# Copying y of the first two units on ScalarE alone, and putting back products that only the next half needs

## The chip, the cores and the metric

The kernel runs on one core of a Trainium2 chip. A core has TensorE (PE, matrix products, with its weight loads listed as PEld), VectorE (DVE), ScalarE (ACT), GpSimd (POOL) and SyncE (SP, which here only issues DMAs). Each works through its own queue in order; semaphores tie the queues together. The metric is the device time in microseconds (us), the median of the runs.

## The reference

A gated linear attention, and behind it a bilinear feed-forward layer. The attention has batch 4, 8 heads, 768 tokens and head size 48:

```python
f = 1.0 / (1.0 + np.exp(-f_logit))
for t in range(S):
    state = f[:, :, t, :, None] * state + np.einsum('bhd,bhe->bhde', k[:, :, t], v[:, :, t])
    y[:, :, t] = np.einsum('bhd,bhde->bhe', q[:, :, t], state)
x = y.transpose(0, 2, 1, 3).reshape(B * S, H * D)
out = ((x @ w_a) * (x @ w_b)) @ w_out
```

x has 3072 rows of 384 channels, and w_a, w_b are 384 x 1536, w_out 1536 x 384. The weights come in as doubles and are turned into 32-bit floats on the chip.

## The kernel before

**Units.** The attention is cut into 16 units: 4 batches, 2 halves of 384 tokens each, 2 groups of 4 heads. Units 0 and 1 (FIRST) are the two head groups of the first half of batch 0; unit 2 and 3 are the same heads in the second half. A unit is cut into chunks of 128 tokens (c from 0 to 2, for n of 2 pairs of heads), and each chunk into two pieces of 64 (p is 0 or 1). Step j = 2c + p goes from 0 to 5.

**Stages of a unit.** The front (front_parts, L313) has four parts: two sigmoids on ScalarE and an affine step on GpSimd; running products of f by a scan on VectorE (L333, one per n) with a small comparison; running sums of the inverse by six scans (L346); and k and q multiplied by them (L350). Then on TensorE: scores (L396), turn (L421, a transpose of k, copied by ScalarE in turned), gains (L445, what each piece adds to the state, one PSUM bank for each p), within (L504, y from the same piece) and across (L530, y from the state before the piece). VectorE masks the scores (L409) and adds up states from the gains (carry, L472 and L474). out_of_bank (L553) copies y out of PSUM, and stores_of (L575) sends it by DMA into xT, the transposed input of the feed-forward part. For unit 0 these stores alternate between SP's and POOL's queues, for unit 1 (u == NQ - 1) they go round ACT, SP and POOL.

Step j = 5 of carry makes the state behind the last piece. Only the next half of the same heads reads it, by way of hand_on, which comes after up(0, 1) in program order.

**The feed-forward part.** up(blk, ft) is 6 calls, 12 matmul records, of x with 128 columns of w_b and w_a (L619). Each call of a 32-bit matmul shows as two records with two weight loads. product copies one factor on ScalarE (L640) and multiplies on VectorE (L645). up(0, 0, True) goes by tiles of xT: the first needs unit 0 alone, the second both units, the third unit 1.

**Weights.** Pieces of the weights are loaded by SP (load_weights, L269) and converted by from_double: begin puts two passes on ScalarE (L71, L72), one on GpSimd (L73), and then a third on ScalarE (L75); end puts the last on VectorE (L78, and L83 three times for w_a and w_b). up(0, 0) needs pieces 0 and 1, up(0, 1) and up(0, 2) pieces 2 and 3, up(0, 3) and up(0, 4) pieces 4 and 5.

**The order.** The head of the kernel, up to the end of unit 3, is written out by hand (L1030 to L1148): every call puts its instructions on the queues in program order. The rest is placed by a planner that works from fixed costs and doesn't see the head. PSUM is ps_x, ps_y (two banks each, one tile for both) and four single banks ps_f, given out by the list idle. turn of a FIRST unit takes two of them, carried gives them back after its last step, and up takes two. keep_up issues products with no use, to a bank that is free.

In the head before, unit 1's within takes two ps_f banks, y of unit 1 is copied in four parts that alternate between ScalarE and VectorE (line 552), and the first scan of unit 2 stands ahead of y of unit 1, the second behind it (L1075 to L1081).

Of the kernel before, what the change touches and what calls it, by code (L numbers as in the profile page):

```python
# [22 lines left out]
BLK = 384  # L23
# [6 lines left out]
R = 64  # L30
SUB = 64
# [78 lines left out]
def kernel(  # L110
# [29 lines left out]
    with ExitStack() as pools:  # L140
        again, ending = by_quotients(pools, tc, q, k, f_logit, v, moe_w_a, moe_w_b, moe_w_out, out, ident, weights, bad, banks)
# [12 lines left out]
def by_quotients(ctx, tc, q, k, f_logit, v, moe_w_a, moe_w_b, moe_w_out, out, ident, weights, bad, ps_f):  # L154
    nc = tc.nc
    B, H, D, S = q.shape
# [4 lines left out]
    NQ = H // 4  # L161
    NC = BLK // C
    NJ = BLK // SUB
# [5 lines left out]
    FIRST = range(NQ)  # L169
# [42 lines left out]
    def unit(u):  # L212
        b, r = divmod(u, NH * NQ)
        return (b, *divmod(r, NQ))
# [57 lines left out]
    def begin(n):  # L272

        while 2 * n > begun[0] < 2 * len(todo):
            i, second = divmod(begun[0], 2)
            dst, src, shape = todo[i]
            if not second:
                going.append(
                    from_double(
                        nc, dst, raws[i], shape[0], next(blocks), bits[i % len(bits)], some, whole, shape[0] == NKT  # L280
                    )
                    if src.dtype != FP32 else iter(())
                )
            next(going[i], None)
            begun[0] += 1
# [19 lines left out]
    live = {}  # L305
    firsts = groups[:, len(EARLY)].rearrange("p (u n s) -> p u n s", u=NQ, n=2)
    products_of_f = {u: firsts[:, u] if u in FIRST else sets[u % NSET]["f"] for u in range(NU)}
# [52 lines left out]
    ps_x, ps_y = (ps_a.tile([128, 2, 512], FP32, tag=n, name=n) for n in ("ps_x", "ps_y"))  # L360
    idle = list(range(4))
# [5 lines left out]
    def each():  # L367
        for n in range(2):
            for c in range(NC):
                yield n, c, (n * NC + c) * SUB  # L370

    def give_back(ps):
        idle.extend(i for x in ps for i, bank in enumerate(ps_f) if bank is x)


    def home(u):

        return ps_y if u in (1, 3) else ps_x
# [5 lines left out]
    def pair_of(x):  # L384

        return [x[:, i] for i in range(2)]
# [17 lines left out]
    def mask(u):  # L404

        at = sb1.tile([128, 2, BLK], FP32, tag="at", name="at")
        to, x = (y.rearrange("s h (o t) -> s h o t", t=SUB) for y in (at, home(u)[:, :, 0:BLK]))
        tri = causal.unsqueeze(1).unsqueeze(1)
        nc.vector.tensor_tensor(to, x, tri.broadcast_to((128, 2, 2 * NC, SUB)), ALU.mult)  # L409
        live[u]["at"] = at  # L410
# [18 lines left out]
        else:  # L429
            nc.scalar.copy(kT.rearrange("s n c x -> s n (c x)"), away(u)[:, :, 0:NC * (R + D)])  # L430

    def gains(u, chunks=range(NC)):

        _, half, _ = unit(u)
        t, kT = sets[u % NSET], live[u]["kT"]
        last = half == NH - 1
        ps = live[u]["turned"]
        for n in range(2):
            for c in chunks:
                for p in range(2):  # L440
                    if last and c == NC - 1 and p == 1:
                        continue
                    for h in range(2):
                        r = slice(SUB * p, SUB * p + SUB)
                        nc.tensor.matmul(  # L445
                            ps[p][R * h:R * h + D, (n * NC + c) * D:(n * NC + c) * D + D],
                            lhsT=kT[r, n, c, R * h:R * h + D],
                            rhs=t["v"][r, n, c, h * D:h * D + D],
                            start=True,
                            stop=True,  # L450
                        )
        if chunks[0]:
            return
        st = sb3.tile([128, NJ, 2, D], FP32, tag="st", name="st")
        before = live[u - NQ]["st"][NJ] if half else None
        live[u]["st"] = [before] + [st[:, j] for j in range(NJ - 1 if last else NJ)]

    def carried(u, js=range(NJ)):

        for j in js:  # L460
            if j + 1 < len(live[u]["st"]):
                carry(u, j)
        if js[-1] == NJ - 1:
            give_back(live[u]["turned"])

    def carry(u, j):

        before, st = live[u]["st"][j:j + 2]
        c, p = divmod(j, 2)
        new = live[u]["turned"][p][:, 0:2 * NC * D].rearrange("r (n c d) -> r n c d", n=2, c=NC)[:, :, c]  # L470
        if before is None:
            nc.vector.tensor_copy(st, new)  # L472
        else:
            nc.vector.tensor_tensor(st, before, new, ALU.add)  # L474
# [16 lines left out]
    def within(u):  # L491

        t, at = sets[u % NSET], live[u]["at"]
        if u == NQ - 1:

            ps = live[u]["y"] = [ps_f[idle.pop(0)] for _ in range(2)]
        else:
            ps = live[u]["y"] = pair_of(home(u) if u < 2 * NQ else ps_y)
        for n, c, o in each():
            for p in range(2):  # L500
                for h in range(2):
                    r = slice(SUB * p, SUB * p + SUB)
                    e = R * (p ^ h)
                    nc.tensor.matmul(  # L504
                        ps[p][e:e + D, o:o + SUB],
                        lhsT=t["v"][r, n, c, h * D:h * D + D],
                        rhs=at[r, h, o:o + SUB],
                        start=o == 0,
                        stop=True,
                        skip_group_check=True,  # L510
                    )

    def across(u):

        b, half, qd = unit(u)
        qf, st, ps = halves(sets[u % NSET]["q"]), live[u]["st"], live[u]["y"]

        order = [(n, c, o, p) for n, c, o in each() for p in range(2)]
        if u in FIRST:

            order = sorted(order[::-1], key=lambda x: -x[3])
        elif half:
            order = [(n, c, o, p) for n, c, o in reversed(list(each())) for p in range(2)]
        for n, c, o, p in order:
            j = 2 * c + p
            if j == half == 0:
                continue
            for h in range(2):
                r, e = slice(R * h, R * h + D), R * (p ^ h)
                nc.tensor.matmul(  # L530
                    ps[p][e:e + D, o:o + SUB],
                    lhsT=st[j][r, n],
                    rhs=qf[r, tokens(n, c, p)],
                    start=False,
                    stop=True,
                    skip_group_check=True,
                )

    def out_of_bank(u, part):

        if "y_sb" not in live[u]:
            if u == NQ - 1:

                live[u]["y_sb"] = groups[:, 2 * NTG - 1, PIECE:].rearrange("r (o p m) -> r o p m", p=2, m=SUB)
            else:
                live[u]["y_sb"] = sb1.tile([128, 2 * NC, 2, SUB], FP32, tag="y", name="y")
        if u == NQ - 1:

            p, e, r, rows = ((1, R, 0, D), (0, 0, 0, D), (1, 0, R, D), (0, R, R, D))[part]
        else:  # L550
            p, e, r, rows = ((1, R, 0, D), (1, 0, R, D), (0, 0, 0, 128))[part if u in FIRST else part - 1]
        copy = nc.vector.tensor_copy if u == NQ - 1 and part % 2 else nc.scalar.copy
        copy(live[u]["y_sb"][r:r + rows, :, p], live[u]["y"][p][e:e + rows, 0:BLK].rearrange("r (o m) -> r o m", m=SUB))  # L553

    def stored(u):

        for do in stores_of(u):
            do()
# [440 lines left out]
    with tc.manual_schedule():  # L999
# [9 lines left out]
        parts = {u: front_parts(u) for u in range(2 * NQ)}  # L1009

        def emit_all(steps):
            for _, _, do, *args in steps:
                do(*args)

        def keep_up(n, to, width=BLK):


            x = products_of_f[0][:, 0, 0:width]
            for _ in range(n):
                nc.tensor.matmul(to[:, 0:width], lhsT=ident, rhs=x, start=True, stop=True)  # L1020

        def y_of(u):
            for part in range(4 if u == NQ - 1 else 3):
                out_of_bank(u, part)
            stored(u)
            if u == NQ - 1:
                give_back(live[u]["y"])


        for u in FIRST:  # L1030
# [30 lines left out]
        emit_all(parts[2][0])  # L1061
        begin(2.5)
        gains(1, range(NC - 1))
        carried(0)
        mask(1)
        carried(1, range(1))

        within(1)
        gains(1, range(NC - 1, NC))
        across(0)  # L1070
        keep_up(1, ps_y[:, 0], SUB)
        y_of(0)
        end(1)
        carried(1, range(1, NJ - 1))
        first_scan, *scans = parts[2][1]  # L1075
        emit_all([first_scan])
        across(1)
        keep_up(2, ps_y[:, 0])
        y_of(1)
        carried(1, range(NJ - 1, NJ))  # L1080
        emit_all(scans)  # L1081
        begin(3)
        end(2)
        emit_all(parts[2][2])


        load_unit(3, "f")
# [600 lines left out]
```

## Time and profile before

| | |
|---|---|
| runs | 589.22, 589.61, 590.11 us; median 589.61 |
| profiled execution | 590.78 us, its span 588.9 us |
| PE busy | 568.4 us, 97% of the span |
| PEld busy | 510.7 us, 87% |
| DVE busy | 412.0 us, 70% |
| ACT busy | 257.5 us, 44% |
| POOL busy | 90.4 us, 15% |
| head, 20.00 to 40.34 us | PE busy 14.97 us, DVE 16.12, ACT 13.87 of 20.34 |
| 40.34 us to the end | PE busy 544.27 of 548.56 us |

The span runs from the first to the last instruction of one profiled execution. In a line of a timeline the first number is the start in us from the span's start, the second the duration, then engine, source line, operation, what is written and read, and how many records are merged. In brackets stands the idle time of the engine ahead of it, and what ended it; "issue" means that the profile shows nothing that the engine waited for. A q behind an engine's name is its sequencer, which issues DMAs.

### The profile page before, as it was taken

What the parts mean: (1) busy time and instruction counts of PE and PEld (TensorE: products, weight loads), DVE (VectorE), ACT (ScalarE), POOL (GpSimd) and SP (SyncE); (2) the same over time, 40 slices, a digit from 0 to 9 for tenths busy, and PEclk for the clock granted to TensorE, in tenths of its full rate; (3) what the DMA queues carried; (4) which work ended last, traced back from release to release, by engine and by line L of the source; (5) the groups of instructions that cost most, each with busy time, mean ns of one, the idle gap of its engine ahead of it and who ended that gap; (6) DMA issues with size and microseconds to landing.
All of it is one profiled execution on the core that took longest, in us unless ns stands there. A gap on an engine that the chain in (4) does not pass through costs nothing.

```text
span 588.9 us, 13930 instructions
## 1 busy us (share of the span) xinstructions
PE 568.4 (97%) x5796; PEld 510.7 (87%) x5796; DVE 412.0 (70%) x782; ACT 257.5 (44%) x494; POOL 90.4 (15%) x73
## 2 busy tenths in 40 slices
PE   2789999999999999999999999999999999999997
PEld 1546655558999999999999999999999999999997
DVE  6799644599878869876997777837785165836651
ACT  5587668652122554246520444326431345235400
POOL 7365456454000000000000000000000000000000
PEclk9999999999999999999999999999999999999999
DMA  8789489089444123034105400041001100000001
GB/s 198 200 237 303 133 241 297 20 151 186 102 133 107 52 53 102 1 90 100 43 2 129 119 11 2 2 113 36 3 1 48 48 2 0 2 28 0 1 29 32
DMA packets 33576, 49.42 MB, mean 84 GB/s; under 512 B 3984, under 2 KB 25280, under 8 KB 33504
## 3 DMA queue, kind: packets, MB, share of 16 engines
q1 hardware_dynamic: 30000, 42.19, 26.2%
q0 software_dynamic: 3088, 5.92, 5.9%
q8 instruction: 47, 0.77, 0.6%
q10 hardware_dynamic: 416, 0.34, 0.2%
q14 instruction: 25, 0.20, 0.1%
HBM read 33.23 MB, written 4.72 MB: 64 GB/s over the span
## 4 chain that ended last, share of the span: by engine, by line
PE 91%; DVE 5%; issue 2%; ACT 1%; DMA 1%; SPq 0%; DVEq 0%; ACTq 0%
PE ps_f L745 39%; PE ps_f L847 28%; PE ps_f L619 15%; PE ps_y L504 2%; PE ps_y L530 2%; PE ps_x L445 1%; PE ps_x L396 1%; PE ps_x L421 1%; DVE inv L346 1%; DVE q_in L350 1%; DVE groups L333 1%; DMA f_in<-in_f_logit_dram 1%; DVE at L409 0%; DVE groups L737 0%; DVE spare L346 0%
## 5 line engine op out<-in xcount | busy, mean ns | idle before, releaser
L619 PE MATMUL ps_f<-xT,w_ba 128*128 128x384 f32 x288 | 95.8, 490 | 0.7 <-DVE w_ba L83 0.6
L1335 ACT COPY sums<-ps_f 128x384 f32<-128x384 f32 x120 | 57.6, 480 | 76.2 <-PE ps_f L745 68.5
L619 PEld LDWEIGHTS ps_f<-xT,w_ba 128*128 128x128 f32 x288 | 53.7, 190 | 37.8 <-ACT spare L75 1.2
L1335 ACT COPY groups<-ps_f 128x384 f32<-128x384 f32 x120 | 57.6, 481 | 61.3 <-PE ps_f L745 40.7
L745 PE MATMUL ps_f<-xT,w_ba 128*128 128x192 f32 x384 | 78.5, 327 | 0.0
L745 PEld LDWEIGHTS ps_f<-xT,w_ba 128*128 128x128 f32 x384 | 64.7, 190 | 0.3
L73 POOL TENSOR_SCALAR sums<-sums 128x768 f32<-128x768 f32 (+1 forms) x20 | 52.6, 2629 | 34.5 <-ACT sums L71 34.4
L745 PE MATMUL ps_f<-groups,w_ba 128*128 128x192 f32 x288 | 54.9, 326 | 0.0
L745 PE MATMUL ps_f<-x_sums,raw 128*128 128x192 f32 x288 | 53.7, 330 | 0.5 <-DVE groups L737 0.5
L329 POOL TENSOR_SCALAR inv<-inv 128x768 f32<-128x768 f32 x14 | 13.6, 972 | 261.2 <-ACT inv L326 217.0
L847 PE MATMUL ps_f<-w_out,sums 128*128 128x192 f32 x288 | 51.9, 327 | 0.0
L847 PE MATMUL ps_f<-w_out,groups 128*128 128x192 f32 x288 | 51.8, 329 | 0.0
L847 PE MATMUL ps_f<-spare,sums 128*128 128x192 f32 x288 | 49.5, 327 | 0.0
L745 PEld LDWEIGHTS ps_f<-x_sums,raw 128*128 128x128 f32 x288 | 47.0, 190 | 2.6 <-ACT sums L1335 1.0
L745 PEld LDWEIGHTS ps_f<-groups,w_ba 128*128 128x128 f32 x288 | 48.0, 190 | 0.1
L847 PEld LDWEIGHTS ps_f<-w_out,groups 128*128 128x128 f32 x288 | 47.2, 190 | 0.7
L847 PEld LDWEIGHTS ps_f<-w_out,sums 128*128 128x128 f32 x288 | 47.3, 190 | 0.2
L847 PEld LDWEIGHTS ps_f<-spare,sums 128*128 128x128 f32 x288 | 47.0, 190 | 0.1
L737 DVE TENSOR_TENSOR sums<-ps_f,sums 128x384 f32<-128x384 f32 x60 | 32.7, 553 | 16.9 <-PE ps_f L745 12.9
L737 DVE TENSOR_TENSOR sums<-sums,groups 128x768 f32<-128x768 f32 x36 | 34.3, 953 | 11.8 <-ACT groups L1335 11.2
L745 PE MATMUL ps_f<-xT,raw 128*128 128x192 f32 x192 | 39.4, 328 | 0.2 <-ACT groups L1335 0.2
L745 PE MATMUL ps_f<-x_sums,w_ba 128*128 128x192 f32 x192 | 39.3, 327 | 0.0
(150 smaller groups left out, 850.7 us busy)
## 6 DMA issues: line engine op xcount, KB each, us to landing
raw<-w_ba POOLq DMA_DIRECT2D x11, 512.0 KB, 8.3
k_in<-in_k_dram SPq DMA_DIRECT2D x32, 144.0 KB, 4.4
q_in<-in_q_dram SPq DMA_DIRECT2D x32, 144.0 KB, 4.5
v_in<-in_v_dram SPq DMA_DIRECT2D x16, 288.0 KB, 5.1
raw<-in_moe_w_out_dram SPq DMA_DIRECT2D x6, 768.0 KB, 4.8
out_dram<-o SPq DMA_DIRECT2D x22, 192.0 KB, 1.9
f_in<-in_f_logit_dram SPq DMA_DIRECT2D x28, 144.0 KB, 3.0
xT<-y SPq DMA_DIRECT2D x44, 72.0 KB, 2.1
```

The source lines that it names most:

```text
L73: nc.gpsimd.tensor_scalar(h, h, HI_MIN, HI_MAX, ALU.max, ALU.min)
L329: nc.gpsimd.tensor_scalar(inv, inv, EXP_K, 1.0, ALU.mult, ALU.add)
L333: nc.vector.tensor_tensor_scan(F[:, c], F[:, c], none, math.exp(MIDDLE), ALU.mult, ALU.add)
L346: nc.vector.tensor_tensor_scan(inv[:, w], inv[:, w], none[:, 0:C], first, ALU.mult, ALU.add)
L350: nc.vector.tensor_tensor(halves(t[nm]), halves(t[nm]), by, ALU.mult)
L504: nc.tensor.matmul(ps[p][e:e + D, o:o + SUB], lhsT=t["v"][r, n, c, h * D:h * D + D], rhs=at[r, h, o:o + SUB], start=o == 0, stop=True, ski ...
L530: nc.tensor.matmul(ps[p][e:e + D, o:o + SUB], lhsT=st[j][r, n], rhs=qf[r, tokens(n, c, p)], start=False, stop=True, skip_group_check=True,)
L619: nc.tensor.matmul(ps[nm][:, 0:BLK], lhsT=w[:, kt, ft * 128:ft * 128 + 128], rhs=xT[blk][:, kt], start=kt == 0, stop=kt == NKT - 1,)
L737: nc.vector.tensor_tensor(to, x, y, op)
L745: nc.tensor.matmul(ps[:, g], lhsT=sums_of_w[name][:, g, 128 * j:128 * j + 128], rhs=sums_of_x[blk][name], start=start and g == 0, stop=Tru ...
L847: nc.tensor.matmul(to, lhsT=x[:, i // 2, i % 2], rhs=w[:, NI * (i % 2) + i // 2], start=start and i == 0, stop=i == HFT - 1, skip_group_ch ...
L1335: do(*args)
```

## The change

Four edits, all in the head:

- Unit 1's within writes ps_y instead of two ps_f banks. Its y is copied in three parts, all on ScalarE, as unit 0's is: first the two parts with 48 rows of bank p = 1, then the 128 rows of bank p = 0.
- The gains of unit 1's last chunk are split by p. Those of p = 0 stay; those of p = 1, which feed step j = 5 alone, go behind across(1). gains gets an argument for it.
- The last carry of unit 0 goes behind the scans of unit 2, the last carry of unit 1 behind the third part of unit 2's front.
- VectorE does both scans of unit 2 in one go, ahead of across(1) in program order. The single keep_up product between across(0) and y of unit 0 is gone; the two behind across(1) now come after y of both units and write a ps_f bank.

```diff
-    def gains(u, chunks=range(NC)):
+    def gains(u, chunks=range(NC), halves=range(2)):
...
-                for p in range(2):
+                for p in halves:
...
     def within(u):
...
-        if u == NQ - 1:
-
-            ps = live[u]["y"] = [ps_f[idle.pop(0)] for _ in range(2)]
-        else:
-            ps = live[u]["y"] = pair_of(home(u) if u < 2 * NQ else ps_y)
+        ps = live[u]["y"] = pair_of(home(u) if u < 2 * NQ else ps_y)
...
-        if u == NQ - 1:
-
-            p, e, r, rows = ((1, R, 0, D), (0, 0, 0, D), (1, 0, R, D), (0, R, R, D))[part]
-        else:
-            p, e, r, rows = ((1, R, 0, D), (1, 0, R, D), (0, 0, 0, 128))[part if u in FIRST else part - 1]
-        copy = nc.vector.tensor_copy if u == NQ - 1 and part % 2 else nc.scalar.copy
-        copy(live[u]["y_sb"][r:r + rows, :, p], live[u]["y"][p][e:e + rows, 0:BLK].rearrange("r (o m) -> r o m", m=SUB))
+        p, e, r, rows = ((1, R, 0, D), (1, 0, R, D), (0, 0, 0, 128))[part if u in FIRST else part - 1]
+        nc.scalar.copy(live[u]["y_sb"][r:r + rows, :, p], live[u]["y"][p][e:e + rows, 0:BLK].rearrange("r (o m) -> r o m", m=SUB))
...
-        def keep_up(n, to, width=BLK):
+        def keep_up(n, to):
...
-            for part in range(4 if u == NQ - 1 else 3):
+            for part in range(3):
                 out_of_bank(u, part)
             stored(u)
-            if u == NQ - 1:
-                give_back(live[u]["y"])
...
         gains(1, range(NC - 1))
-        carried(0)
+        carried(0, range(NJ - 1))
         mask(1)
         carried(1, range(1))
 
         within(1)
-        gains(1, range(NC - 1, NC))
+        gains(1, range(NC - 1, NC), range(1))
         across(0)
-        keep_up(1, ps_y[:, 0], SUB)
         y_of(0)
         end(1)
         carried(1, range(1, NJ - 1))
-        first_scan, *scans = parts[2][1]
-        emit_all([first_scan])
+        emit_all(parts[2][1])
         across(1)
-        keep_up(2, ps_y[:, 0])
+
+        gains(1, range(NC - 1, NC), range(1, 2))
         y_of(1)
-        carried(1, range(NJ - 1, NJ))
-        emit_all(scans)
+        carried(0, range(NJ - 1, NJ))
+        keep_up(2, ps_f[idle[-1]])
         begin(3)
         end(2)
         emit_all(parts[2][2])
+        carried(1, range(NJ - 1, NJ))
```

More of the change, by code (lines that the diff above doesn't have):

```diff
@@ L1013, in emit_all @@
                 do(*args)
-        def keep_up(n, to, width=BLK):
-            x = products_of_f[0][:, 0, 0:width]
+        def keep_up(n, to):
+            x = products_of_f[0][:, 0]
             for _ in range(n):
-                nc.tensor.matmul(to[:, 0:width], lhsT=ident, rhs=x, start=True, stop=True)
+                nc.tensor.matmul(to[:, 0:BLK], lhsT=ident, rhs=x, start=True, stop=True)
         def y_of(u):
-            for part in range(4 if u == NQ - 1 else 3):
+            for part in range(3):
                 out_of_bank(u, part)
             stored(u)
-            if u == NQ - 1:
-                give_back(live[u]["y"])
         for u in FIRST:
```

## The prediction

> **What bounds the kernel now.** I read the page first: TensorE (PE) is busy for 97% of the span, VectorE (DVE) for 70%, ScalarE (ACT) for 44%. Then the waits of PE over the whole run. After the first 10.4 us (the start) only a few are left, and nearly all lie in the head, before 41 us:
>
> ```profile
> PE ps_f L1020 <- POOL ident masks.py:199: 10.4, 1, 10.4
> PE ps_x L530 <- issue: 2.3, 1, 2.3
> ...
> PE ps_x L396 <- DVE q_in L350: 0.7, 1, 0.7
> PE ps_f L619 <- DVE w_ba L83: 0.6, 1, 0.6
> PE ps_y L421 <- DVE k_in L350: 0.6, 1, 0.6
> ```
>
> The table by stretches says the same: from 40.34 to the end PE is busy 544.27 of 548.56 us. So what the head gains before the up product at 40.34 moves everything behind it, and what it gains elsewhere is worth nothing. Next, PE's timeline around the change (start, duration, instruction, count, idle before):
>
> ```profile
> 22.69 0.56 PE L445 MATMUL ps_f<-v_in,kT 64*48 64x48 f32 x28 [0.35 <-issue]
> 23.34 0.89 PE L504 MATMUL ps_f<-at,v_in 64*48 64x64 f32 x48
> 24.05 0.36 PE L445 MATMUL ps_f<-v_in,kT 64*48 64x48 f32 x16
> 24.23 1.01 PE L530 MATMUL ps_x<-q_in,st 48*48 48x64 f32 x36
> 27.52 0.32 PE L530 MATMUL ps_x<-q_in,st 48*48 48x64 f32 x4 [2.27 <-issue]
> 27.76 0.43 PE L1020 MATMUL ps_y<-groups,ident 128*128 128x64 f32 x2
> 28.13 1.90 PE L530 MATMUL ps_f<-q_in,st 48*48 48x64 f32 x40
> 29.95 2.40 PE L1020 MATMUL ps_y<-groups,ident 128*128 128x384 f32 x4
> 32.30 0.88 PE L619 MATMUL ps_f<-xT,w_ba 128*128 128x384 f32 x2
> 33.77 3.46 PE L619 MATMUL ps_f<-xT,w_ba 128*128 128x384 f32 x10 [0.59 <-DVE w_ba L83]
> ```
>
> PE stops for 2.27 us inside across(0) (L530), four records short of its end, and waits for no engine. Between the pause of 0.35 us and this one lie 28+48+16+36 = 128 matmul records; each has its weight load, so exactly 256 instructions. In that pause the DMA view has one packet of a queue called "instruction" with 0.02 MB. I read it as PE waiting for its next block of instructions.
>
> The same moments on DVE:
>
> ```profile
> 25.66 0.95 DVE L333 TENSOR_TENSOR_SCAN f_in<-f_in,zero 128x384 f32<-128x384 f32 x1
> 30.10 1.14 DVE L553 COPY groups<-ps_f 48x384 f32<-48x384 f32 x2 [3.49 <-PE ps_f L530]
> 31.27 0.26 DVE L474 TENSOR_TENSOR st<-st,ps_f 128x96 f32<-128x96 f32 x1
> 31.44 0.95 DVE L333 TENSOR_TENSOR_SCAN f_in<-f_in,zero 128x384 f32<-128x384 f32 x1
> ```
>
> DVE stands still for 3.49 us: in order, its copies of y(1) wait for across(1), and the second scan of unit 2 is queued behind them. From there the chain of waits is DVE's until 40.30 (scans, conversion of the first w_a piece, scans of inv, k, q, next conversion), where PE's up(0,1) takes over at 40.34.
>
> [...] the granted clock is 0.60 in 28.00:32.30, and across(1) takes 1.90 us for 40 records, where across(0) did 36 in 1.01. [...] The stores of y land 2.0 to 2.5 us after issue.
>
> **The change part by part.**
>
> 1. *Gains of the last chunk's second half move behind across(1)*: 4 calls, 8 records with 8 loads, 16 instructions. The block boundary stays where it is, 128 records after the pause at 22.69: rest of the gains 28, within 48, gains 8, across(0) 40 make 124. So across(0) now ends 4 records before the boundary, at about 24.1 + 0.95 = 25.05, and the stop falls two calls into across(1). across(1) can't start earlier than 25.74 anyway (its state carries end there on DVE). The block arrives at 27.52 as before[...]. 36 records then take 0.82 us as at 24.23, the last few at low clock: across(1) ends near 28.6 (before: 30.03). The moved gains cost 0.15 there: 28.75.
>
> 2. *keep_up(1) goes*: 0.36 us of PE, all of it in front of across(1), counted already. keep_up(2) stays but targets a bank of unit 0's gains; it waits for the deferred carry, which DVE does at 27.6 to 27.9, earlier. Its records took 0.80, 0.64 and then 0.44 as the clock came back at 31.68. Starting at 28.75 in the slow clock: 0.80 + 3 x 0.64, end near 31.5 (before 32.30). Without the slow clock 4 x 0.33 would end it at 30.1; both ends meet again in step 5.
>
> 3. *y(1) in ps_y, three copies on ACT*: before, two on ACT and two on DVE. Cost on ACT one more of 0.48; on DVE minus 1.14. ps_y is one tile: y(0)'s copies from the one tile ps_x waited for all of across(0) (27.87), so I let y(1)'s wait for all of across(1): 28.65 to 30.1 (before the last DVE copy ended at 31.24). y(0)'s copies are long done then: 25.1 to 26.55, its five stores on SP and POOL issued by 28.5, not 31.2.
>
> 4. *y(1)'s stores* stay on ACT, SP, POOL, ACT, SP: from 30.15, issues of 0.5 to 0.77, the last at 30.85 (before 31.88); with 2.5 us landing at 32.65 for the first and 33.35 for the last. Behind them on SP are the loads of unit 3 and the next weights, on POOL the clearing of f; all come about 1.0 us earlier. On ACT the last sign pass (L75) of piece 2 comes at 31.55, before 32.19: only 0.65 us earlier, as ACT was never much ahead.
>
> 5. *up(0,0)*: starts 31.5, first tile of xT 1.35 us; second tile has landed at 32.65, so no wait; 12 records at 0.325 and a slow first: end 35.5 (before 37.23). With a warm clock it would start at 30.1, wait for 32.65, and end at 32.65 + 8 x 0.325 = 35.25. The choice hardly matters.
>
> 6. *DVE*: second scan at 26.54 instead of 31.44. Taking its own durations on: hold 27.5, deferred carry 27.6, conversion of w_a piece 0 until 29.1, restart and six scans 2.86 us to 31.96, carry of unit 1 to 32.25, k until 33.2, q until 34.1 (34.7 if POOL's conversion is in its way, as in the 1.58 us at 37.67). That is 4.65 us ahead: the 3.49 idle plus 1.14 of copies. The deferred carries feed only hand_on, which ACT does after 37: free. turn(2) and scores(2) find k and q ready, and run straight behind up(0,0): 35.5 + 0.6 + 0.9 = 37.0.
>
> 7. *up(0,1)* needs pieces 2 and 3 converted. DVE can begin them at 34.7 and needs 1.15 to the first third of piece 2: 35.9, in time. Piece 3 waits for ACT and POOL: L71 ends 33.5 on ACT, POOL 2.8 more, 36.3; first third 37.4, needed at 37.0 + 2.0. In time.
>
> So PE is at up(0,1) at 37.0 instead of 40.34: **3.3 us**. Behind that PE's order rules and ACT follows PE. The tightest place is up(0,3): piece 5's first third is ready at 51.6 before, needed near 52.8, slack 1.2. ACT comes only 0.85 us earlier there, PE 3.3, but DVE's own queue was the later one then; POOL ends at 47.3, first third 48.4, needed at 49.4. Slack 1.0. The profiled execution then has a span of 588.9 - 3.3 = 585.6 and 590.78 - 3.3 = 587.5 in all; it lies 1.17 above the median, so for the median 589.61 - 3.35 = 586.3, rounded to 586.2.
>
> **The rivals.**
>
> *A, forecast (0.62)*: 2.8 to 4.0 us gained, 585.6 to 586.8. Should the boundary still fall in across(0), y(0)'s copies start at 27.87 and y(1)'s end at 30.75: 0.65 later, 586.9, so A's edge.
>
> *B, part is given back in the conversions (0.14)*: ACT moves 0.65 to 0.85 us, PE 3.3; if the slack of 1.0 at up(0,3) is not there, PE waits for POOL there. For it: POOL's 2.8 to 3.2 us passes hang on ACT's order. Against: ACT was idle 3.98 us at 46.9. It costs 1 to 2: 587.3 to 588.3.
>
> *C, more is gained (0.11)*: DVE's whole 4.65 reaches PE, if copies overlap across(1), the block comes earlier and PE stays warm: 585.0.
>
> *D, nothing measurable (0.08)*: the gain is lost in waits for weights by 100 us, where DMA is at its limit (share 1.05 in 80:100). Against: ACT's waits there are for PE. 589.3.
>
> *E, ScalarE sets the end (0.05), slower*: ACT alone copies y(1), then issues two stores, then converts. It is level with before when across(1) ends at 29.3, and past 30.5 (plus the 1.2 slack) pieces 4 and 5 delay PE beyond before. If the block came 3.4 us later, at 30.9, across(1) would end at 32.0 and the kernel at 591.1. [...]
>
> **How the numbers follow.** A change within 0.2% (1.2 us) is about what can't be told from none. Faster: A, B and C, 0.87; same: D, 0.08; slower: E, 0.05. A's own range is 585.6 to 586.8; for 8 in 10, most of B and C come in: 584.9 to 588.0.
>
> **What would show it.** Right: three ACT copies of y(0) near 25.1; a pause without an engine's name four records into across(1), ending near 27.5; no DVE idle of over 1 us between 25 and 34; ACT's y(1) copies ending near 30.1; up(0,0) without a wait for L83; up(0,1) near 37.0; PE without gaps behind. Wrong: a pause before the end of across(0), copies that wait longer, or PE idle at up(0,1) or up(0,3) behind L83.

## The result, and the profile after

| | before | changed |
|---|---|---|
| median of 16 runs each, measured in turn | 590.33 us | 588.95 us |
| ratio of the runs | | 0.9965, 95% interval 0.9951 to 0.998 |
| profiled execution, and its span | 590.78, 588.9 us | 588.95, 587.1 us |
| start of up(0,1) in the profile | 40.34 us | 37.05 us |
| end of the last product | 585.56 us | 582.31 us |
| from the last product to the end | 3.37 us | 4.79 us |

The change makes the kernel faster by about 0.35%, some 2.1 us. The forecast was 586.2 us, with 584.9 to 588.0 as its range: right in the sign, too large in the size. The ratio goes with the means of the 16 runs, 591.03 and 588.92 us, which lie 2.11 apart; the medians lie only 1.38 apart, and the repetition below agrees with the ratio.

The waits of TensorE in the changed kernel (us in total, times, longest), to set beside those of before:

```profile
PE ps_f L1010 <- POOL ident masks.py:199: 10.4, 1, 10.4
PE ps_f L610 <- DMA xT<-y: 1.6, 1, 1.6
PE ps_y L526 <- issue: 1.1, 1, 1.1
...
PE ps_y L526 <- DVE st L474: 0.6, 1, 0.6
```

The pause without an engine's name has gone down from 2.3 to 1.1 us and has moved from ps_x, which is across(0), to ps_y, which is across(1). The waits for k, q and converted weights ahead of up(0,1) are gone; what is left is a wait of 1.6 us of up(0,0) for a store of y.

TensorE's timeline of the changed kernel around the change:

```profile
24.21 1.11 PE L526 MATMUL ps_x<-q_in,st 48*48 48x64 f32 x39
25.90 0.32 PE L526 MATMUL ps_y<-q_in,st 48*48 48x64 f32 x4 [0.58 <-DVE st L474]
27.32 0.87 PE L526 MATMUL ps_y<-q_in,st 48*48 48x64 f32 x30 [1.10 <-issue]
...
28.46 1.56 PE L1010 MATMUL ps_f<-groups,ident 128*128 128x384 f32 x4
31.58 4.11 PE L610 MATMUL ps_f<-xT,w_ba 128*128 128x384 f32 x12 [1.56 <-DMA xT<-y]
35.52 0.74 PE L421 MATMUL ps_y<-ident,k_in 112*128 112x112 f32 x6
36.19 0.93 PE L396 MATMUL ps_x<-q_in,k_in 48*64 48x64 f32 x48
37.05 4.14 PE L610 MATMUL ps_f<-xT,w_ba 128*128 128x384 f32 x12
```

across(0) runs through. The pause comes exactly four records into across(1) and ends at 27.32, where before it ended at 27.52. From up(0,0) on nothing stands between the groups.

VectorE's timeline of the changed kernel:

```profile
25.02 0.83 DVE L474 TENSOR_TENSOR st<-st,ps_f 128x96 f32<-128x96 f32 x3
25.77 1.80 DVE L333 TENSOR_TENSOR_SCAN f_in<-f_in,zero 128x384 f32<-128x384 f32 x2
27.60 0.16 DVE L336 TENSOR_TENSOR held<-f_in,least 128x2 f32<-128x2 f32 x1
27.68 0.25 DVE L474 TENSOR_TENSOR st<-st,ps_f 128x96 f32<-128x96 f32 x1
...
31.21 0.95 DVE L350 TENSOR_TENSOR k_in<-k_in,inv 128x768 f32<-128x768 f32 x1
32.08 0.95 DVE L350 TENSOR_TENSOR q_in<-q_in,f_in 128x768 f32<-128x768 f32 x1
```

The two scans are one line now, and the idle time of 3.49 us in front of the copies is gone with the copies. k and q of unit 2 are finished at 33.0, well ahead of their use at 35.5 and 36.2.

And ScalarE's copies of y, before:

```profile
27.87 1.45 ACT L553 COPY y<-ps_x 48x384 f32<-48x384 f32 x3 [4.10 <-PE ps_x L530]
29.60 0.97 ACT L553 COPY groups<-ps_f 48x384 f32<-48x384 f32 x2 [0.28 <-PE ps_f L530]
```

and in the changed kernel:

```profile
25.39 1.45 ACT L544 COPY y<-ps_x 48x384 f32<-48x384 f32 x3 [1.57 <-PE ps_x L526]
28.43 1.45 ACT L544 COPY groups<-ps_y 48x384 f32<-48x384 f32 x3 [1.58 <-PE ps_y L526]
29.90 1.24 ACTq L566 DMA_DIRECT2D xT<-groups  x2
31.19 1.16 ACT L75 ACTIVATE spare<-raw,some 128x768 f16<-128x768 f32 x1 [1.31 <-issue]
```

So this head is what was forecast, step by step, and the last product ends 3.25 us earlier than in the profile of before. Two things then don't agree with a gain of 2.1: these profiled heads, and the last line of the table, where the changed kernel needs 1.42 us more after its last product. The experiments are about these two, and about which part of the change does the work.

### The profile page after: what moved, and what is told of

Same layout as the page of the kernel before. It is cut to its first block, busy times and chain, and to the rows that moved or that the text cites. A ratio compares the mean times of both kernels' runs of the same rounds, so it can differ in the third digit from the quotient of the medians.

```text
span 587.1 us, 13926 instructions
## 1 busy us (share of the span) xinstructions
PE 566.4 (96%) x5794; PEld 510.3 (87%) x5794; DVE 409.9 (70%) x780; ACT 258.2 (44%) x495; POOL 91.0 (16%) x73
## 3 DMA queue, kind: packets, MB, share of 16 engines
q0 software_dynamic: 3088, 5.92, 5.9%
## 4 chain that ended last, share of the span: by engine, by line
PE 92%; DVE 4%; DMA 1%; issue 1%; ACT 1%; SPq 0%; DVEq 0%; ACTq 0%
PE ps_f L736 39%; PE ps_f L838 28%; PE ps_f L610 16%; PE ps_y L500 2%; PE ps_y L526 2%; PE ps_x L396 2%; PE ps_x L445 1%; PE ps_x L421 1%; DVE q_in L350 1%; DMA xT<-y 1%; DVE groups L333 1%; DVE inv L346 1%; DMA f_in<-in_f_logit_dram 1%; DVE groups L728 0%; DVE spare L346 0%
```

## The experiments

"Up(0,1)" is the start of its first product in the profiled execution, "end" the time from the last product to the end of the span. Ratios are to runs of the kernel before on the same chip at the same time, with 95% intervals. "Mean span" is over all executions of a kernel, "se" the standard error of a mean or of a difference.

### Both kernels again

Both kernels unchanged:

> The kernel before, unchanged, to see how far executions of one kernel lie apart and whether its end always looks as in the first profile (3.37 us from the last product to the end of the span). Theory 'late end' (the head's 3.3 us hold, and what is missing of them is lost behind the last product[...]): ratio 1.000, up(0,1) at 40.3, the end 3.4 us or, in some executions, near 4.8. Theory 'clock' (half-clock windows of TensorE fall on work that now sets the pace): the same ratio, but a half-clock window between 25 and 35 us in nearly every execution, at no cost here, because VectorE sets the pace until 40.3.

> The changed kernel, unchanged. 'Late end': up(0,1) again near 37.0 and the last product 3.2 to 3.4 us earlier than before; ratio 0.9945 if the end is 3.4 us, 0.997 if it is 4.8. 'Clock': spans of executions with a mean clock of 1.000 some 1 to 2 us shorter than those with 0.993 to 0.996.

Measured: before 0.9999 (0.9987 to 1.0012), up(0,1) at 40.34, end 4.80 us. Changed 0.9966 (0.9951 to 0.998), up(0,1) at 37.20, end 4.82. The gain repeats. The end of 3.37 us in the first profile of before doesn't: with 4.80 there, that span would have been 590.4 and not 588.9.

### One part alone, and one part undone

*y of unit 1 on ScalarE alone*, nothing else of the change; the keep_up products go to a free ps_f bank, as ps_y holds y:

```diff
-        if u == NQ - 1:
-            ps = live[u]["y"] = [ps_f[idle.pop(0)] for _ in range(2)]
-        else:
-            ps = live[u]["y"] = pair_of(home(u) if u < 2 * NQ else ps_y)
+        ps = live[u]["y"] = pair_of(home(u) if u < 2 * NQ else ps_y)
...
-        keep_up(2, ps_y[:, 0])
+        keep_up(2, ps_f[idle[-1]])
```

> The kernel before with one edit: y(1) in ps_y and copied in three parts by ScalarE; gains, carries, scans and keep_up in their old order (keep_up on a ps_f bank, since ps_y is taken). VectorE no longer waits for across(1). If the VectorE wait was the whole cost, as the forecast's step 6 has it: up(0,1) as early as in the changed kernel, 37.1. If TensorE's own way decides (across(1) to 30.0, copies to 31.5, stores landed by 34.0): up(0,0) ends near 36.7 and up(0,1) starts at 38.2, so 2.1 us of the 3.3 and ratio 0.9975; the other edits then bring 1.2.

Measured: 0.9974 (0.996 to 0.9988), mean span 588.26 against 589.42 of before beside it. Its timeline of TensorE:

```profile
28.28 0.32 PE L526 MATMUL ps_x<-q_in,st 48*48 48x64 f32 x4 [2.90 <-issue]
...
33.05 4.43 PE L610 MATMUL ps_f<-xT,w_ba 128*128 128x384 f32 x12
37.31 0.74 PE L421 MATMUL ps_y<-ident,k_in 112*128 112x112 f32 x6
37.98 0.93 PE L396 MATMUL ps_x<-q_in,k_in 48*64 48x64 f32 x48
38.84 3.49 PE L610 MATMUL ps_f<-xT,w_ba 128*128 128x384 f32 x10
```

The pause ended only at 28.28, and the clock was low behind it (2.91 us for keep_up's four records, 1.56 in the changed kernel), yet up(0,1) came at 38.84. VectorE began k at 31.40 (36.80 in before), and the three waits for k, q and a converted weight, 1.9 us together in before, are gone. About 1.2 us (se 0.35), something like half of the whole gain, is this edit alone.

*The changed kernel without the split of the gains*:

```diff
-        gains(1, range(NC - 1, NC), range(1))
+        gains(1, range(NC - 1, NC))
...
-        gains(1, range(NC - 1, NC), range(1, 2))
```

> The changed kernel, with all gains of unit 1's last chunk ahead of across(0) again. By the prediction (step 1 and rival A): the pause moves into across(0), 4 records before its end; y(0)'s copies start at about 27.6 instead of 25.39, y(1)'s end near 30.6 instead of 29.88, up(0,1) 0.5 to 0.7 us later, at 37.6. Rival: y(0)'s stores wait until 31.5 in the changed kernel too[...]; then the split is worth nothing, and up(0,1) stays within 0.2 us of 37.1.

Measured: 0.9986 (0.9974 to 0.9997), mean span 588.72. TensorE's timeline of this kernel:

```profile
24.19 1.01 PE L526 MATMUL ps_x<-q_in,st 48*48 48x64 f32 x36
26.98 0.26 PE L526 MATMUL ps_x<-q_in,st 48*48 48x64 f32 x2 [1.78 <-issue]
...
28.07 1.56 PE L1010 MATMUL ps_f<-groups,ident 128*128 128x384 f32 x4
31.77 5.92 PE L610 MATMUL ps_f<-xT,w_ba 128*128 128x384 f32 x12 [2.14 <-DMA xT<-y]
```

The pause is back in across(0), four records before its end, as in the kernel before. ScalarE's copies of y(0) start at 27.33 and not at 25.39, its copies of y(1) end at 30.25, and up(0,0) waits 2.14 us for a store. On top the clock halves at 33.06, so up(0,0) takes 5.92 us in place of 4.11, and up(0,1) comes at 39.05. Of the 2.00 us that it lies behind the first profile of the changed kernel, 0.19 are a later start of up(0,0) and 1.81 the half clock. Over many executions the split is worth about 1.5 us of mean span (588.72 against 587.27, se 0.3), more than the 0.5 to 0.7 that I had given it. The edit decides where the pause falls: in before and in the changed kernel it comes 128 matmul records behind the pause before it (0.35 us at 22.69, 0.45 us at 22.77), and with 16 instructions fewer ahead of across(0) that is past its end. How much of the 1.5 us is the later stores, and how much a half clock, one profile doesn't show. All edits but the split gain 0.70 us on the kernel before (se 0.3), no more than the first one alone, so the moved carries and scans show no gain of their own.

*VectorE takes half of the copies again*, all else changed: y(1) from ps_y in four parts, alternately.

```diff
...
-        nc.scalar.copy(...)
+        copy = nc.vector.tensor_copy if u == NQ - 1 and part % 2 else nc.scalar.copy
+        copy(...)
...
-            for part in range(3):
+            for part in range(4 if u == NQ - 1 else 3):
```

> The changed kernel, but y(1) is copied in four parts that ScalarE and VectorE take in turn (VectorE behind its scans): so the order of the changed kernel without 'ScalarE alone'. VectorE gets 1.1 us more, and has 1.0 us of slack at 36.16, where it waits for GpSimd. Copies end 0.3 to 0.5 us earlier. If ScalarE alone is what frees VectorE: up(0,1) 1 us later or more. If the order of the scans is what counts: up(0,1) within 0.3 us of 37.1, ratio as the changed kernel's.

Measured: 1.0007 (0.9994 to 1.002). The whole gain is gone. VectorE's timeline of this kernel:

```profile
28.14 0.55 DVE L548 COPY groups<-ps_y 48x384 f32<-48x384 f32 x1 [0.38 <-ACT groups L548]
29.23 0.56 DVE L548 COPY groups<-ps_y 48x384 f32<-48x384 f32 x1 [0.54 <-ACT groups L548]
29.82 0.25 DVE L474 TENSOR_TENSOR st<-st,ps_f 128x96 f32<-128x96 f32 x1
```

and TensorE's:

```profile
30.13 2.34 PE L1014 MATMUL ps_f<-groups,ident 128*128 128x384 f32 x4 [2.39 <-DVE st L474]
32.26 4.99 PE L614 MATMUL ps_f<-xT,w_ba 128*128 128x384 f32 x12
37.09 0.74 PE L421 MATMUL ps_y<-ident,k_in 112*128 112x112 f32 x6
37.76 0.93 PE L396 MATMUL ps_x<-q_in,k_in 48*64 48x64 f32 x48
38.62 3.81 PE L614 MATMUL ps_f<-xT,w_ba 128*128 128x384 f32 x11
```

The copies of the two engines wait for each other, one after the other: the four parts take 2.16 us, where three on ScalarE alone take 1.45. The last carry of unit 0 is behind them at 29.82 (27.68 in the changed kernel), and TensorE's keep_up, whose bank it frees, waits 2.39 us for it; the clock is low from 30.77 to 34.18 (2.34 us for keep_up's four records, 1.56 in the changed kernel), and up(0,1) comes at 38.62. VectorE reaches k at 33.88 in place of 31.21, but in this profile that costs nothing: k and q are finished at 34.8 and 35.7, ahead of their use at 37.09 and 37.76. So VectorE must be free of these copies, as forecast, but what is seen to be late here is the carry, and not k and q as in before.

### The clock

Before has a stretch at half clock that begins inside across(1): the granted clock is 0.50 from 28.27 to 31.68 in the first profile. If that is the loss, a head without it should be faster. The kernel before with two more products with no use, ahead of across(0), to fill the pause:

```diff
+        keep_up(2, ps_y[:, 0])
         across(0)
```

> The kernel before with two idle products (keep_up(2, ps_y[:, 0]), 1.3 us at full clock) ahead of across(0). They end at about 25.5, across(0) at its boundary near 26.4, the instruction block still arrives at 27.2 to 27.5: so they fit into the wait and change no dependence. Theory 'clock' (in both profiles of the kernel before, across(1) ran in a half-clock window, 1.9 to 2.0 us instead of about 1.0, and VectorE's copies, which set its pace, waited for it; executions without that window are about 1 us shorter, and the forecast took the slow head for the usual one): no half-clock window over across(1), its 40 records in 1.0 us, up(0,1) near 39.4 instead of 40.34, mean time 0.4 to 0.9 us below the kernel before. Theory 'late end': across(1) may be quicker, but the time is that of before within 0.2 us.

Measured: 1.0001 (0.9986 to 1.0016), although in the profiled execution across(1) ran at full clock (1.15 us for 40 records) and up(0,1) was at 38.64. TensorE did not pause there, and still waited for VectorE's converted weights: 2.43 us ahead of up(0,0), 0.74 ahead of up(0,1). The changed kernel with three and with four products behind across(1), where it has two:

```diff
-        keep_up(2, ps_f[idle[-1]])
+        keep_up(3, ps_f[idle[-1]])
```

> Changed kernel with keep_up(3) for keep_up(2): 4 more TensorE instructions, so as many as the kernel before has, put where TensorE idles 1.56 us (30.02 to 31.58). Costs nothing before 31.58 if the clock is full. 'Late end', if the count of instructions places the last block: the end is 3.4 us again as before, span 585.6. If only chance places it: either value. 'Clock': half of the idle time is filled, fewer half-clock windows.

> Changed kernel with keep_up(4): the idle time of 1.56 us is filled by 1.3 us of products. 'Clock': no half-clock window after 31 us in any execution, the spread of spans shrinks to that of the kernel before, and the median falls by 0.5 to 1 us against the changed kernel. 'Late end': no change of the median by more than 0.5 us except through where the last block falls.

Measured: 0.9947 (0.9925 to 0.9969; eight executions) and 0.9971 (0.9958 to 0.9984). Their profiles have up(0,1) at 36.76 and 36.31, better than the changed kernel, and their times are not distinguishable from its 0.9965. In three kernels, then, a profiled head that was 0.3 to 1.7 us better than the first one of the kernel it was made from was not measurably better over many executions. That the full clock explains the gain is not borne out.

### More heads of each kernel

This led to the question how far one profiled head stands for a kernel. Both unchanged, profiled again:

> The kernel before, unchanged: one more profiled head. Theory 'untypical head' (the two profiles of before, both with up(0,1) at 40.34, are slower in the head than most executions, whose span is 589.4 on average): up(0,1) falls between 38.6 and 40.3, by the time at which the instruction block behind record 128 arrives and whether TensorE falls to half clock, and the last product ends 545.1 to 545.3 later. Theory 'typical head' (40.3 each time; what is lost lies elsewhere in the run): up(0,1) at 40.2 to 40.4 here too, and the span varies behind it.

> As the look before it: up(0,1) spread over 38.6 to 40.3, mean near 39.5, if the first two profiles were untypical; 40.2 to 40.4 if they were typical.

> As the two looks before it. The pause in TensorE's across(0) ends between 26.5 and 28.3; up(0,1) follows it by some 12.5 to 13 us where across(1) runs at half clock, and by some 11.5 where it runs at full clock.

> The changed kernel, unchanged: a third profiled head. Both theories: up(0,1) at 36.8 to 37.6 (37.05 and 37.20 so far), since VectorE's scans no longer wait for across(1); 4.8 us from the last product to the end.

> The kernel before, unchanged: a sixth profiled head and end. So far up(0,1) at 40.34, 40.34, 39.23, 38.84, 41.04 and 4.8, 4.8, 4.6, 3.4, 3.3 us from the last product to the end. Theory 'the heads were untypical': up(0,1) below 40. Theory 'the end': 3.3 or 4.8 to the end, the short end being found in before only.

> The changed kernel, unchanged: a fourth profiled head and end. up(0,1) at 36.6 to 37.4. If the short end is as likely as in the kernel before (2 of 5), one of this and the next look should show 3.3 us to the end; if the change has lost it, both show 4.8 to 5.2.

> The changed kernel, unchanged: a fifth profiled head and end, with the same expectations as the look before it: up(0,1) at 36.6 to 37.4; 3.3 us to the end if the short end is left to chance, 4.8 to 5.2 if the change has lost it.

Measured, with the first profiles and the repetitions (us):

| kernel | up(0,1) | end of the last product | end | span |
|---|---|---|---|---|
| before | 40.34 | 585.56 | 3.37 | 588.9 |
| before | 40.34 | 585.33 | 4.80 | 590.1 |
| before | 39.23 | 584.55 | 4.80 | 589.3 |
| before | 38.84 | 584.13 | 3.30 | 587.4 |
| before | 41.04 | 586.39 | 4.59 | 591.0 |
| before | 40.20 | 585.56 | 4.62 | 590.2 |
| **mean of 6** | **40.00** | **585.25** | **4.25** | **589.5** |
| changed | 37.05 | 582.31 | 4.79 | 587.1 |
| changed | 37.20 | 582.43 | 4.82 | 587.2 |
| changed | 36.62 | 582.03 | 5.14 | 587.2 |
| changed | 37.10 | 583.04 | 4.65 | 587.7 |
| changed | 37.19 | 582.62 | 5.52 | 588.1 |
| **mean of 5** | **37.03** | **582.49** | **4.98** | **587.5** |

The gain at up(0,1) is 2.97 us between the means (se 0.35), at the last product 2.76 (se 0.37), at the end 2.03. Over all executions of the two kernels the mean spans are 589.36 (199) and 587.27 (34): 2.09 with a standard error of 0.21. So the five and six profiles, unlike the first pair, add up to what the runs say. The head of before spreads over 2.2 us, that of the changed kernel over 0.6.

What spreads before's head can be seen in the profiles with the earliest and the latest up(0,1). TensorE's timeline of the earliest:

```profile
26.67 0.32 PE L530 MATMUL ps_x<-q_in,st 48*48 48x64 f32 x4 [1.44 <-issue]
...
27.28 1.15 PE L530 MATMUL ps_f<-q_in,st 48*48 48x64 f32 x40
```

and of the latest:

```profile
27.72 0.45 PE L530 MATMUL ps_x<-q_in,st 48*48 48x64 f32 x4 [2.56 <-issue]
...
28.73 1.99 PE L530 MATMUL ps_f<-q_in,st 48*48 48x64 f32 x40
```

The pause, which I read as the wait for a block of instructions, ends 1.05 us later in the second, and across(1) runs at half clock, 1.99 us in place of 1.15. The table by stretches for 24 to 26 us shows what the DMA engines did meanwhile (the last two columns are their share and GB/s); first the early, then the late one:

```profile
24.00:26.00 2.00, 1.24 (x69) 1.14 (x60) 1.86 (x9) 0.00 (x0) 1.85 (x1) 1.00 0.04 13
```

```profile
24.00:26.00 2.00, 1.16 (x64) 1.06 (x53) 1.86 (x9) 0.00 (x0) 1.90 (x1) 1.00 0.51 88
```

In the early one the loads of weights and units were through at 24 us (share 0.04), in the late one they kept the DMA engines half busy (0.51). Over the 17 profiles whose loads were issued as in before, the start of the block's packet (23.64 to 25.71 us; 16 KB, on the queue that the DMA view calls instruction) goes with the bytes moved from 22 to 26 us (295 to 594 KB), with a correlation of 0.74. Four of the six heads of before have a stretch at half clock around across(1) and up(0,0) and lie at 40.20 to 41.04; the two without lie at 38.84 and 39.23. The changed kernel has such a stretch in two of five, with up(0,1) at 37.20 and 37.10: there it costs nothing that can be seen.

### What the block of instructions waits for

If it waits behind the loads, 288 KB less in front should bring it earlier. The changed kernel with the q loads of unit 2 behind y(0)'s stores on SP:

```diff
         load_unit(2, "k")
-        load_unit(2, "q")
...
         y_of(0)
+        load_unit(2, "q")
```

> The changed kernel with unit 2's two q loads (288 KB) issued on SP behind y(0)'s stores, at about 28.7 us, where before they were the last of the loads that fill the DMA queues until 24 to 25. Theory 'the block waits behind the loads': at some 385 GB/s the 288 KB are 0.75 us, so the packet of the block starts near 24.0 instead of 24.6 to 24.9, the pause in across(1) ends near 26.6 instead of 27.3, keep_up ends 0.5 to 0.7 earlier, up(0,1) is at 36.4 to 36.8, and the time is 0.3 to 0.7 us below the changed kernel (ratio 0.995 to 0.996), if the q load, which then lands near 31.9, is there for VectorE's use of it at 32.1. Theory 'the block comes at a fixed time after the block before it': packet at 24.6 to 24.9 and pause end at 27.3 as before, time as the changed kernel or 0.5 to 1 slower through the q load.

Measured: the packet starts at 23.98 (24.30 to 24.88 in the five profiles of the changed kernel), and the pause in across(1) is 0.28 us and ends at 26.57. The table by stretches of this kernel, for 22 to 24 us, shows the DMA engines nearly free, with a share of 0.28 (1.00 in the changed kernel):

```profile
22.00:24.00 2.00, 1.56 (x97) 1.31 (x90) 1.65 (x4) 1.90 (x3) 1.17 (x2) 1.00 0.28 54
```

And yet the packet is no earlier than in four profiles with all loads in place (23.64 to 23.99). So here the loads don't seem to be what it waited for. The ratio is 1.0009 (0.9995 to 1.0022). VectorE's and TensorE's timelines of this kernel show the price:

```profile
34.10 0.96 DVE L350 TENSOR_TENSOR q_in<-q_in,f_in 128x768 f32<-128x768 f32 x1 [1.87 <-DMA q_in<-in_q_dram]
```

```profile
30.64 1.53 PE L610 MATMUL ps_f<-xT,w_ba 128*128 128x384 f32 x4 [1.02 <-DMA xT<-y]
34.30 2.82 PE L610 MATMUL ps_f<-xT,w_ba 128*128 128x384 f32 x8 [2.14 <-DMA xT<-groups]
```

The load was issued at 29.9, later than the 28.7 of my expectation, landed 2.2 us after the 31.9 I had for it, and the stores of y(1) on the same queue were late with it. The block was earlier, and the gain was lost twice over.

The same loads on ScalarE's own queue, ahead of y(0)'s copies, with two and with three products behind across(1):

```diff
-        load_unit(2, "q")
...
+        load_unit(2, "q", nc.scalar)
         y_of(0)
```

> The changed kernel with unit 2's two q loads issued on ScalarE's own DMA queue just ahead of y(0)'s copies, where ScalarE stands idle from 23.8 to 25.4. Theory 'the block waits behind the loads': as with the loads moved behind y(0)'s stores, the packet starts near 24.0 and the pause ends near 26.6, but the q load lands near 28 and stands in nobody's way: up(0,0) at 30.6, up(0,1) at 36.2 to 36.6, against 37.0 (mean of the five profiles of the changed kernel), and a time 0.4 to 0.8 below the changed kernel's, ratio 0.9952 to 0.996. Rival 'a load on another queue is ahead of the block all the same': pause end 27.3 or later, up(0,1) at 37.0, ratio 0.9965 or above.

> The same with three records of keep_up where the changed kernel has two, the variant that was fastest so far (0.9947, eight executions). If an early block and a warm clock each help: ratio 0.994 to 0.995. If TensorE now waits for the stores of y instead, it is at the same time as with two records, 0.9952 to 0.996.

Measured: 0.9963 (0.995 to 0.9976) and 0.9972 (0.9959 to 0.9985). The first one's timeline of TensorE:

```profile
26.88 0.87 PE L526 MATMUL ps_y<-q_in,st 48*48 48x64 f32 x30 [0.59 <-issue]
...
31.05 4.11 PE L610 MATMUL ps_f<-xT,w_ba 128*128 128x384 f32 x12 [1.44 <-DMA xT<-y]
...
36.53 4.14 PE L610 MATMUL ps_f<-xT,w_ba 128*128 128x384 f32 x12
```

The block came earlier again (packet at 24.09; 24.06 in the second one, with up(0,1) at 36.05), as expected, although ScalarE's queue issued these loads at 21.3 and not at 23.8. So in all three kernels the packet started earlier than in any of five profiles of the changed one. But it did so too in the two with more products behind across(1) (23.90 and 23.80), which leave the loads alone. The packet was later where more bytes moved (the 0.74 above); that moving the loads made it early here isn't beyond chance. The time hardly follows: up(0,0) waits for the stores of y instead, and with mean spans of 586.67 and 587.59 against 587.27 no version is clearly better than the changed kernel.

## Why the prediction was wrong

**Right: the mechanism.** What it named as visible in the profile is there.

| step | forecast | first profile after | five profiles |
|---|---|---|---|
| 1. pause four records into across(1), end | 27.52 | 27.32 | 26.9 to 27.5 |
| 1. copies of y(0) start | 25.1 | 25.39 | |
| 1. across(1) and the moved gains end | 28.75 | 28.5 | |
| 2. keep_up ends | 31.5 | 30.0 | |
| 3. copies of y(1) end | 30.1 | 29.88 | |
| 5. up(0,0) ends | 35.5 | 35.7 | |
| 6. up(0,1) starts | 37.0 | 37.05 | mean 37.03 |

keep_up ended 1.5 us earlier as the clock wasn't low (1.00 in 28.00:32.30, where before had 0.60), and step 5 had said that this hardly matters: up(0,0) then waits for the stores, here until 31.58. VectorE began k 5.6 us earlier than before (36.80 to 31.21), where step 6 has 4.65 (its own times, 36.80 and 32.25, give 4.55); nothing waited for it. It has no idle time above 1 us from 25 to 34, and up to up(0,1) only one, 1.04 us at 36.16 for POOL's pass of a weight piece, which delays no product.

**Wrong: the sum.** It was "span of 588.9 - 3.3 = 585.6", and for the median "589.61 - 3.35". The step that failed is this subtraction: it took the gain of one profiled head for the kernel's, and let all of it reach the end. Over all executions the mean span falls by 2.09 us (se 0.21). In the profiles three terms were off.

- *The head that it subtracts from.* 40.34 is one execution. Six have a mean of 40.00, so 0.34 us of the 3.3 would be that execution's late block and low clock; the six heads scatter so much that this mean has a standard error of 0.33. I had treated the arrival at 27.52 and the half clock as properties of the kernel, when they vary by more than a microsecond from one execution to the next.
- *Nothing is lost behind up(0,1).* On average 0.21 us is (2.97 to 2.76), most of it in one profile. This one has 0.44 us without an engine's name near up(0,3), inside across(2); another profile has 0.44 near 148 us. That is no conversion that is late, so rival B didn't happen.
- *What lies after the last product stays as it is.* I carried over the profiled 3.37 us without asking whether it was usual. It is 3.3 or 4.6 to 4.8 in before, and 4.6 to 5.5 in the changed kernel: 0.73 us more on average. Together 0.34 + 0.21 + 0.73 is 1.28, and the forecast's 3.3 less 1.28 is the 2.0 of the profiles, as it must be: the terms split the difference up and don't prove it.

The last term, the largest, isn't settled. The short end is in two of six profiles of before and none of five of the changed kernel, but also in two kernels made from the changed one (3.31 and 3.32 with the moved q loads); the other seven of the variants have 4.7 to 5.2. With such counts the 0.73 (se 0.32) may be chance. The mean spans should then differ by what the last product gains, 2.76 (se 0.37), and they differ by 2.09 (se 0.21): that is not far enough off to decide.

**The base.** Apart from the gain, 589.61 was the median of three runs; sixteen have 590.33. Of the 2.75 us between forecast and result, 0.72 are this, and the other 2.03 the smaller gain (the forecast has 3.41 between its base and 586.2, the medians have 1.38).

**The rivals.** C's case, an earlier block and TensorE at full clock (1.56 us for four records of keep_up, 2.20 for six), is what the profiles with the q loads on ScalarE's queue have: up(0,1) came at 36.05 and 36.53, near C's gain, but over many executions it wasn't kept. What A gave to a boundary left in across(0), "0.65 later", was less than half of it: undoing the split costs 1.5 (se 0.3). D's and E's signs were not seen: no wait for weights, and ScalarE at 29.9 is 0.2 earlier than forecast.

**The pause without an engine's name.** Here it is 1.4 to 2.6 us in the six profiles of before, and 0.5 to 1.2 in those of the changed one. Elsewhere there is little of it: the first profile of before has 47 packets of the queue called instruction, 0.77 MB in all, and 11592 instructions of TensorE (5796 products, 5796 weight loads), and the list of TensorE's waits has, besides this pause, only two more without an engine's name, of 0.4 and 0.2 us.

## What to carry to other kernels

A forecast from one profile needs the spread of that profile's own landmarks: profile the unchanged kernel a few times, and subtract from the mean of the stretch, above all where it holds a pause that no engine explains, and look at the end of the run as well as at the place of the change. Where an engine pauses and the profile names nothing that it waited for, count its instructions since the pause before: here there were 256 in both kernels, and moving 16 that nobody needed yet to behind the pause put it where it delayed less, for about 1.5 us (se 0.3). The copy shared by two engines was slower here, as its parts waited for each other (2.16 us, against 1.45 on ScalarE alone); on ScalarE, which was idle anyway (1.58 us ahead of these copies), it freed VectorE for the work that set the pace.

## What the runs showed that was not expected

**The block of instructions comes late where the loads do.** Its packet started between 23.64 and 25.71 us, later on the whole where more bytes were moved around it (correlation 0.74), and where TensorE paused it went on 2.3 to 3 us after its start. How much of that is the queue and how much is its own time stays open.

**The end of the run has two lengths.** In the DMA view of the last stretch, from 582 us on in the changed kernel and from 585 us on in before, the two last stores take (KB each, median us to landing):

```profile
out_dram<-w_ba SPq DMA_DIRECT2D x2, 96.0 KB, 2.6
```

```profile
out_dram<-w_ba SPq DMA_DIRECT2D x2, 96.0 KB, 2.0
```

In the changed kernel's profile the last nine packets of the store start only from 2.35 us after the last product on, just as a 16 KB packet of the queue called instruction ends, which had lasted from 1.48 to 2.36. In before's profile the store's last packet had ended at 1.81, before the packet of instructions started at 1.90. The other traces agree: in all 16 with a long end, nine packets of the store come late, the first of them within 0.02 us of the end of such a packet; in the four with the short end none comes late. The packet started at 1.10 to 1.48 in 15 of the long ends (2.20 in the longest), and at 1.57 to 2.02 in the short ones. Why the two go together was not shown: no run moved the packet of instructions.

**Half clock isn't always a cost.** Heads of the kernel before with such a stretch have up(0,1) 1.4 us later (40.5 on average against 39.0), partly because the block was later in them too. In the changed kernel the two heads with it are as early as those without, as up(0,0) waits for the stores in any case: in the repetition keep_up's four records took 2.89 us in place of 1.56, and up(0,0) started at 31.54, against 31.58 in the first profile.

**Pauses of nearly the same length went with either clock.** TensorE's pause in across(0) was 1.75 us in the repetition of before, and across(1) behind it took 1.99 us for its 40 records; it was 1.80 us in the profile with up(0,1) at 39.23, and across(1) took 1.15. With 1.44 us (up(0,1) at 38.84) across(1) took 1.15, with 2.27 us in the first profile 1.90, and with 2.56 us (up(0,1) at 41.04) 1.99. What decides between the two, with a pause of 1.75 to 1.80 us, was not shown.
